# Gated linear attention into an ELU layer: a 48-column stationary operand in k·v, and a new issue order for the first ten spans

## The chip, the cores and the metric

One core of one Trainium2 chip. The metric is the time of one launch in device microseconds. Its engines are named as in the profile: PE (matmul) with its weight loads PEld, DVE, ACT, POOL, and SP, which here only issues DMAs.

## The reference

```python
for t in range(S):                    # B, H, S, D = 4, 8, 768, 48, float32
    state = alpha[:, :, t, :, None] * state + np.einsum('bhd,bhe->bhde', k[:, :, t], v[:, :, t])
    y[:, :, t] = np.einsum('bhd,bhde->bhe', q[:, :, t], state)
x = y.transpose(0, 2, 1, 3).reshape(3072, 384)
h = x @ w_in                          # w_in 384 x 2048
g = np.where(h > 0.0, h, np.exp(np.minimum(h, 0.0)) - 1.0)
out = g @ w_out                       # w_out 2048 x 384
```

## The kernel before

**Attention.** Each of the 4 batches is cut into 6 spans of 128 steps (`W`), 24 spans i in all, and each span into two chunks of 64 steps. The 8 heads lie as 4 pairs; a pair has its two heads on partitions 0 to 47 and 64 to 111. P is the running product of alpha within a span (L209, a scan on DVE), R its reciprocal (by logarithm and exponential on ACT, L218 and L223; a Newton step in L231, L236 and L241). k is divided by P, q multiplied by P. Within a chunk the scores k·q are masked and multiplied by v; across chunks a 48 x 48 state per head carries on. Its update is "k over P times v", called u, and then a multiplication by P.

**The feed-forward layer.** Two spans make a block b of 256 rows (12 blocks), and 256 hidden columns make a group j (8 groups). A group A is 18 matmuls of 128 x 256 (L655), and O is 12 matmuls of 128 x 384 (L706): every factor is split in a high and a low part, and three of the four products are formed.

**Steps and order.** The program is a list of steps; each is a name with its indices, and emits its instructions for whatever engine it uses. Every engine, and SP's DMA queue, works through its own instructions in the order of the list. There are two lists. `START` is written out by hand for spans 0 to 9 (with some steps of 10 and 11) and the first 29 of the 96 groups A. `STEADY` is one list for a group of two spans, repeated with moved indices to the end. The names that matter here, with their lines:

- LA, LB, L, LV, F: loads on SP (alpha; k and q; all three; v; weights).
- SC (L209, DVE scan), LN and EX (ACT), KA (L231) and KB (L236) on DVE or POOL, KC (L241, DVE): k over P. SQ (L258, L261): q times P.
- TP (L282, four 128 x 128 transposes on PE) with KN (L311, ACT copy) for spans 0 to 5; TA, TB, T (L292, 16, 16 and 8 transposes of 32 x 128 on DVE) from span 6 on: k with time on the partitions.
- S (L346; L330 from span 6 on): scores. MK (L363; L358): mask, on DVE.
- U (L392; L374, in the function U4, from span 6 on): u. U4 has 16 matmuls, each with one quadrant (64 x 64) of the array; the profile shows each as two records. The last span of a batch needs only half of them.
- UA, UB (L409 on ACT, L411 on DVE) and UC (L440, L442 on DVE): the state update. UP (L418): a subtraction on PE.
- YL, Y3, Y (L453, L458, L486, L497): y. XH (ACT), XP (L516, PE), XL (L534, L538 on DVE; ACT for spans 0 and 1), XD: y in two parts, the x of the next layer.
- DA (L581), DB (L587), DC (L593) on DVE: float64 words of a weight to float32, each 128 x 1536. WH (L619, ACT), WP (L628 and L516, PE), WL (L637 ACT, L639 POOL or DVE): its two parts.
- RA (L663) and RB (L668) on ACT, RC (L673, DVE), GH (L679, ACT), GL (L692, DVE): the ELU of one h and its two parts. Z (L714, L717): a block's output.

All PSUM tiles come from one pool `psa` of eight buffers, handed out in list order. A matmul into a new tile waits until the last reader of the buffer's tile before is done. The h of a group is freed by GL, its last reader.

Of the kernel before, what the change touches and what calls it, by code (L numbers as in the profile page):

```python
# [44 lines left out]


START = """
LA.0 LB.0 SC.0 LN.0 EX.0 LA.1 KA.0 KB.0 LB.1 SC.1 X.2 LV.0 LN.1 X.2 KC.0 F.2 SQ.0 EX.1 F.0 TP.0 KN.0 S.0 U.0
SQ.1 UA.0 KA.1 KB.1 MK.0 L.2 KC.1 UC.0 YL.0 LV.1 TP.1 PC.0 Y3.0 Y.0 KN.1 DA.0 PC.1 LV.2 DB.0 L.3 F.4 S.1 SC.2
U.1 XH.0 F.6 DC.0 UP.1 LN.2 XP.0 EX.2 KA.2 SQ.2 MK.1 UA.1 F.5 WH.0 WP.0 YL.1 F.1 F.3 UC.1 Y3.1 KB.2 SC.3 KC.2  # L50
WH.2 XL.0 PC.2 LN.3 DA.2 EX.3 SQ.3 Y.1 DB.2 KA.3 XH.1 TP.2 WP.2 DC.2 KB.3 KN.2 DA.1 DB.1 XP.1 KC.3 U.2 XL.1
WL.2 LC.0 WL.0 S.2 A.0.0 RA.0.0 WH.6 WL.6 F.7 A.0.1 MK.2 UB.2 UA.2 TP.3 LV.3 UC.2 S.3 L.4 KN.3 F.9 YL.2 U.3
WH.4 SC.4 WL.4 Y3.2 Y.2 UA.3 PC.3 RB.0.0 MK.3 XH.2 DA.3 SQ.4 DC.1 DB.3 YL.3 LN.4 XL.2 Y3.3 UB.3 A.0.2 LV.4
WH.3 EX.4 F.10 CA.0 F.8 WL.3 Y.3 A.0.3 XH.3 UC.3 DC.3 XL.3 L.5 F.12 RA.0.1 KA.4 KB.4 A.1.1 A.1.0 LV.5 F.11
RC.0.0 RB.0.1 RC.0.1 WH.7 GH.0.0 SC.5 DA.5 RA.0.2 GH.0.1 A.1.2 RB.0.2 DB.5 RA.1.0 KC.4 RC.0.2 WH.1 RB.1.0 F.14
GH.0.2 GL.0.0 RC.1.0 WL.1 RA.1.1 GL.0.2 A.1.3 RA.0.3 GL.0.1 RB.0.3 TP.4 UB.0 DA.4 PC.4 RB.1.1 WL.7 WH.5 KN.4
O.0.0 RC.0.3 O.0.1 GH.0.3 DB.4 U.4 WL.5 GL.0.3 RC.1.1 DC.4 RA.1.3 GH.1.1 S.4 LN.5 O.0.2 O.0.3 RB.1.3 DC.5 LV.6
L.6 WH.8 MK.4 UB.4 RA.1.2 EX.5 LV.7 GH.1.0 UA.4 RB.1.2 WL.8 GL.1.0 WH.9 KA.5 RC.1.2 CB.0 A.0.4 GH.1.2 GL.1.1
UC.4 WH.10 KB.5 RA.0.4 KC.5 O.1.0 RC.1.3 TP.5 GL.1.2 SQ.5 GH.1.3 LC.1 DA.6 CA.1 KN.5 WH.11 L.7 O.1.1 DB.6
RB.0.4 WL.10 U.5 PC.5 RC.0.4 GL.1.3 GH.0.4 UA.5 A.1.4 A.0.5 SC.6 RA.1.4 WL.11 LN.6 EX.6 KA.6 WL.9 DC.6 F.15  # L60
RB.1.4 RA.0.5 O.1.2 GL.0.4 WH.14 O.1.3 RC.1.4 RB.0.5 RC.0.5 GH.0.5 GH.1.4 S.5 KB.6 SC.7 KC.6 WH.12 Y.4 O.0.4
WL.12 GL.1.4 PC.6 LN.7 EX.7 WL.14 MK.5 GL.0.5 F.13 A.0.6 TB.6 A.0.7 CB.1 L.8 RA.0.6 A.1.5 DA.7 KA.7 TA.6 DB.7
O.0.5 XH.4 RB.0.6 RA.0.7 ZV.6 RC.0.6 RA.1.5 O.1.4 GH.0.6 XL.4 RB.0.7 Y.5 RB.1.5 KB.7 DC.7 KC.7 GL.0.6 A.1.6
WH.13 WL.13 TB.7 SQ.7 XH.5 WH.15 PC.7 XL.5 RC.0.7 RC.1.5 GH.0.7 LV.8 O.0.6 GL.0.7 TA.7 XD.4 WL.15 RA.1.6 SQ.6
RB.1.6 U.6 O.0.7 UA.6 XD.5 UB.6 UB.1 RC.1.6 GH.1.5 A.1.7 Z.0 GL.1.5 UC.6 GH.1.6 U.7 S.6 UA.7 O.1.5 SC.8 UB.7
MK.6 RA.1.7 LN.8 UC.7 A.2.4 RB.1.7 RA.2.4 GL.1.6 S.7 A.2.1 EX.8 MK.7 A.2.0 RC.1.7 Y.6 RB.2.4 RC.2.4 KA.8
RA.2.1 RB.2.1 Y.7 GH.1.7 RA.2.0 KB.8 KC.8 RB.2.0 RC.2.1 GL.1.7 L.9 SC.9 SQ.9 XH.6 XH.7 RC.2.0 GH.2.0 A.2.3
O.1.6 LN.9 TB.8 XL.7 O.1.7 A.2.5 RA.2.3 LV.10 EX.9 SQ.8 TA.8 GL.2.0 L.10 GH.2.1 KA.9 GL.2.1 U.8 PC.8 XL.6 Z.1
UA.8 S.8 XD.7 RA.2.5 A.2.2 RB.2.3 UB.8 A.2.6 UC.8 RC.2.3 KB.9 MK.8 KC.9 O.2.0 RA.2.2 RB.2.2 GH.2.4 RC.2.2 TA.9
SC.10 GH.2.2 RB.2.5 XD.6 LN.10 A.2.7 GL.2.2 GL.2.4 RA.2.6 RB.2.6 EX.10 O.2.1 RC.2.6 KA.10 GH.2.3 A.3.0 RC.2.5  # L70
RA.2.7 GL.2.3 L.11 O.2.2 LC.2 PC.9 LV.11 KB.10 RA.3.0 TB.9 O.2.3 RB.3.0 KC.10 GH.2.5 RB.2.7 GL.2.5 GH.2.6
O.2.4 RC.2.7 O.2.5 GH.2.7 RC.3.0 GL.2.6 GH.3.0 O.2.6 TA.10 S.9 GL.2.7 GL.3.0 SQ.10 LV.9 MK.9 TB.10 U.9 L.12
UA.9 UB.9 UC.9 SC.11 LN.11 EX.11 SQ.11 A.3.1 RA.3.1 RB.3.1 RC.3.1 GH.3.1 GL.3.1 O.2.7 Z.2 KA.11 KB.11 PC.10
A.3.2 RA.3.2 RB.3.2 RC.3.2 GH.3.2 CA.2 CB.2 LC.3 GL.3.2 O.3.0 KC.11 TA.11 A.3.3 RA.3.3 RB.3.3 RC.3.3 GH.3.3
CA.3 CB.3 LC.4 GL.3.3 O.3.1 TB.11 A.3.4 RA.3.4 RB.3.4 RC.3.4 GH.3.4 GL.3.4 O.3.2
"""


# [10 lines left out]
def gla_elu_ffn(ctx: ExitStack, tc: tile.TileContext, qka, vv, vn, wgt, out):  # L89
    nc = tc.nc  # L90
# [106 lines left out]
    @tok
    def V0(i):
        if EARLY <= i < QU:
            nc.sync.dma_start(out=v0[i % 2][0:64], in_=vv[i, 0:64, HD:2 * HD])  # L200
# [63 lines left out]
    @tok
    def ZS(i):
        if EARLY <= i < QS:
            for a in range(2):
                nc.gpsimd.memset(win[i]["st"][64 - 64 * a:128 - 64 * a, a], 0.0)


    @tok
# [95 lines left out]
    def U4(i):  # L367
        d = win[i]
        q4, begun = shared(i)
        d["u"] = [t[:, 0:NP * D].rearrange("p (n e) -> p n e", n=NP) for t in q4]  # L370
        for n in range(NP):
            for x, a in QUADS if i % NW < NW - 1 else QUADS[::2]:
                r = slice(64 * x, 64 * x + 64)
                nc.tensor.matmul(d["u"][x][64 * a:64 * a + 64, n, :], lhsT=d["kn"][r, n, a, :],  # L374
                                 rhs=d["vn"][r, 2 * n + a, :], start=(n == 0 and x not in begun), stop=True,
                                 skip_group_check=True)
        begun.update((0, 1) if i % NW < NW - 1 else (0,))

    @tok
    def U(i):  # L380
# [4 lines left out]
        d["u"] = [u[:, 0], u[:, 1]]
        m = 64 if i < EARLY else D
        for x in ((1, 0) if i % NW < NW - 1 else (0,)):
            r = slice(0, C) if x == 0 and i < EARLY else slice(0, 128)
            v = d["vn"] if x or i < EARLY else v0[i % 2].rearrange("p (h e) -> p h e", e=D)
            for n in range(NP):  # L390
                for a in range(2):
                    nc.tensor.matmul(d["u"][x][64 * a:64 * a + m, n, :], lhsT=d["kn"][r, n, a, 0:m],  # L392
                                     rhs=v[r, 2 * n + a, :],
                                     start=(x == int(i % NW < NW - 1) and n == 0), stop=True, skip_group_check=True)
# [573 lines left out]
```

## Time and profile before

| what | value |
|---|---|
| median of 3 runs | 504.48 us (504.24 to 504.65) |
| span of the profiled execution | 502.5 us |
| instructions in it | 13254 |
| PE, PEld busy | 98%, 95% |
| DVE, ACT, POOL busy | 77%, 58%, 26% |

The profiled execution's own time is its span and what lies before and after it: the median of the runs is about 2.0 us above the span. A row of a timeline is the start, the duration, the engine, the line, the operation, what it writes and reads, its shape, and, with x32, how many instructions the row joins; the brackets at its end hold the idle time of the engine before it and what ended that. A row of waits has the total, the count and the longest. A row of a group has, behind the first bar, its busy time and the mean ns of one. A row of a chain has only start and duration.

### The profile page before, as it was taken

Reading aid. Unit: us, or ns where it says so; the run is one execution under the profiler, and the core shown is the slowest. Engines: PE = TensorE matmul, PEld = TensorE weight load, DVE = VectorE, ACT = ScalarE, POOL = GpSimd, SP = SyncE. Lnnn points to the kernel's source line nnn. Section 1 sums busy time; section 2 is a strip of 40 time slices with the busy share of each in tenths; the row PEclk is TensorE's granted clock in tenths of the full one; section 3 lists DMA queues with packets and bytes.
Section 4 is the critical chain, followed back from the end, with each engine's and each line's share of the span. In section 5 each row is a group of like instructions: output and inputs, shape, how many; then the busy total and the mean of one; then the engine's idle time right before and its main releaser. Section 6 shows DMA issues by size and latency. Waiting matters only on the chain.

```text
span 502.5 us, 13254 instructions
## 1 busy us (share of the span) xinstructions
PE 492.4 (98%) x5404; PEld 476.0 (95%) x5404; DVE 386.6 (77%) x807; ACT 289.5 (58%) x689; POOL 129.4 (26%) x111
## 2 busy tenths in 40 slices
...
GB/s 311 412 411 382 91 95 165 64 59 100 190 59 64 57 130 178 65 83 219 54 119 178 48 119 182 63 112 172 82 112 97 95 76 44 56 42 8 3 33 36
DMA packets 22403, 61.13 MB, mean 122 GB/s; under 512 B 2880, under 2 KB 9792, under 8 KB 22336
## 3 DMA queue, kind: packets, MB, share of 16 engines
...
q8 instruction: 44, 0.72, 0.6%
...
## 4 chain that ended last, share of the span: by engine, by line
PE 96%; DVE 2%; ACT 1%; issue 1%; ACTq 0%
PE o L706 40%; PE h L655 40%; PE y L458 4%; PE y L453 2%; PE q L374 2%; PE q L330 2%; PE u L392 1%; PE sc L346 1%; PE wp L126 1%; PE y L497 1%; PE tp L282 1%; DVE kn L292 0%; PE yl L453 0%; PE wd L628 0%; DVE st L358 0%
## 5 line engine op out<-in xcount | busy, mean ns | idle before, releaser
L655 PE MATMUL h<-xt,w 128*128 128x256 f32 x1728 | 215.0, 282 | 0.0
L655 PEld LDWEIGHTS h<-xt,w 128*128 128x128 f32 x1728 | 209.3, 188 | 1.8
L706 PE MATMUL o<-w,gh 128*128 128x384 f32 x768 | 199.3, 341 | 0.6 <-ACT gh L679 0.6
L706 PEld LDWEIGHTS o<-w,gh 128*128 128x128 f32 x768 | 136.9, 188 | 1.6 <-ACT gh L679 0.8
L706 PE MATMUL o<-w,gl 128*128 128x384 f32 x384 | 130.0, 339 | 0.1
L679 ACT CAST gh<-h 128x512 fp32r<-128x512 f32 x96 | 55.9, 583 | 79.6 <-DVE h L673 39.3
L692 DVE TENSOR_TENSOR gl<-h,gh 128x512 fp32r<-128x512 f32 x96 | 65.5, 687 | 35.5 <-ACT gh L679 34.2
L292 DVE STREAM_TRANSPOSE kn<-qka 32x128 f32<-32x128 f32 x288 | 87.0, 302 | 4.5
L663 ACT ACTIVATE r<-h 128x512 f32<-128x512 f32 x96 | 57.0, 595 | 47.2 <-PE h L655 40.7
L673 DVE SCALAR_TENSOR_TENSOR h<-r,h 128x512 f32<-128x512 f32 x96 | 64.6, 689 | 16.9 <-ACT r L668 16.1
L706 PEld LDWEIGHTS o<-w,gl 128*128 128x128 f32 x384 | 72.1, 188 | 0.4 <-DVE gl L692 0.4
L231 POOL TENSOR_TENSOR qka<-qka,R 128x512 f32<-128x512 f32 x19 | 26.1, 1375 | 164.6 <-DVE gl L692 127.6
L668 ACT ACTIVATE r<-r 128x512 f32<-128x512 f32 x96 | 59.4, 631 | 0.7
L261 POOL TENSOR_TENSOR st<-qka,P 64x512 f32<-64x512 f32 x36 | 42.8, 1189 | 21.7 <-DVE P L209 16.2
L358 DVE TENSOR_TENSOR st<-q,mask 64x256 f32<-64x256 f32 x72 | 30.4, 422 | 12.0 <-ACT vs L409 9.2
L209 DVE TENSOR_TENSOR_SCAN P<-qka,first 128x516 f32<-128x516 f32 x24 | 30.6, 1275 | 1.6 <-DMA qka<-in_qka_dram 1.2
L236 POOL TENSOR_TENSOR R<-P,R 128x512 f32<-128x512 f32 x20 | 24.2, 1211 | 27.3 <-DVE qka L231 25.9
L218 ACT ACTIVATE R<-P 128x512 f32<-128x512 f32 x24 | 15.2, 632 | 27.8 <-DVE P L209 27.8
L411 DVE TENSOR_TENSOR vs<-vs,q 48x192 f32<-48x192 f32 x30 | 10.5, 350 | 19.1 <-PE q L330 16.9
L511 ACT ACTIVATE y<-y 128x128 fp32r<-128x128 f32 x20 | 5.5, 275 | 30.0 <-PE y L458 26.6
L639 POOL TENSOR_TENSOR w<-spare,w 128x768 fp32r<-128x768 f32 x7 | 15.8, 2256 | 26.0 <-ACT w L619 13.9
L611 ACT ACTIVATE ck<-ck,lim 128x384 f32<-128x384 f32 x32 | 20.6, 644 | 0.1
...
## 6 DMA issues: line engine op xcount, KB each, us to landing
...
```

The source lines that it names most:

```text
L209: nc.vector.tensor_tensor_scan(out=P.rearrange("p n w -> p (n w)"), data0=t[:, 2 * NP * W:], data1=first.rearrange("p n w -> p (n w)"), in ...
L231: eng(KAV, i).tensor_tensor(out=d["kt"], in0=d["kt"], in1=d["R"], op=ALU.mult)
L261: eng(SQV, i).tensor_tensor(out=st[r, a], in0=d["q"][r], in1=pw(i)[r], op=ALU.mult)
L292: nc.vector.transpose(out=kn[32 * t:32 * t + 32, :, 32 * g:32 * g + 32], in_=d["kt"][32 * g:32 * g + 32, :, 32 * t:32 * t + 32])
L358: nc.vector.tensor_tensor(out=d["st"][r, a, :, c * C:(c + 1) * C], in0=d["s4"][a][o], in1=mask[o].unsqueeze(1).broadcast_to([64, NP, C]), ...
L655: nc.tensor.matmul(h[:, f, :], lhsT=t[:, wi, ws], rhs=x[:, c, xi, :], start=(f == 0 and k == 0), stop=(k == 8), skip_group_check=True)
L663: nc.scalar.activation(out=r, in_=d["h"], func=AF.Relu, scale=-1.0)
L668: nc.scalar.activation(out=d["r"], in_=d["r"], func=AF.Exp, scale=-1.0)
L673: nc.vector.scalar_tensor_tensor(out=d["h"], in0=d["r"], scalar=-1.0, in1=d["h"], op0=ALU.add, op1=ALU.max)
L679: nc.scalar.copy(out=gh, in_=d["h"])
L692: nc.vector.tensor_tensor(out=gl, in0=d["h"], in1=d["gh"].bitcast(F32), op=ALU.subtract)
L706: nc.tensor.matmul(o[:, 0:DM], lhsT=gt[:, f, ms], rhs=t[:, wi, f * DM:f * DM + DM], start=(j == 0 and f == 0 and k == 0), stop=(j == NJ - ...
```

## The change

**First**, U4 takes 48 columns of k (0 to D) as its stationary operand, in place of 64, and writes 48 rows of each quadrant in place of 64; rows 48 to 63 of each quadrant hold padding, which no later step reads. **Second**, `START` is a new list of the same steps for the same spans, with a few steps more of spans 10 and 11 in another place. **Third**, the two v0 tiles, with two memsets on POOL, and the code that would use them (for no span, as `EARLY`, `QU` and `QS` are all 6) are removed. Line numbers fall by 1 from the list on and by 10 to 17 later: L209 becomes L199, L231 L221, L241 L231, L292 L275, L374 L357, L392 L375, L411 L394, L442 L425, L581 L564, L587 L570, L593 L576, L655 L638, L673 L656, L692 L675, L706 L689, and L453 L436.

```diff
@@ START @@
-LA.0 LB.0 SC.0 LN.0 EX.0 LA.1 KA.0 KB.0 LB.1 SC.1 X.2 LV.0 LN.1 X.2 KC.0 F.2 SQ.0 EX.1 F.0 TP.0 KN.0 S.0 U.0
...
+LA.0 SC.0 LN.0 LA.1 EX.0 X.2 SC.1 LB.0 KA.0 LB.1 LN.1 KB.0 LV.0 KC.0 X.2 EX.1 KA.1 TP.0 F.2 KN.0 F.0 SQ.0 SQ.1 LV.1
...
+RB.1.4 KN.5 EX.7 A.0.7 L.8 WL.12 RC.1.4 GH.0.5 RA.0.7 A.0.6 DA.7 PC.6 GH.1.4 TA.6 GL.0.5 U.5 RA.0.6 GL.1.4 UA.5
+RB.0.6 DB.7 Y.5 CB.0 RC.0.6 Y.4 DC.7 GH.0.6 XH.4 O.0.5 XH.5 GL.0.6 XL.4 WH.15 XL.5 KA.7 RB.0.7 U.6 RC.0.7 LC.1 KB.7
...
@@ gla_elu_ffn @@
-    v0 = [work.tile([128, HD], F32, name=f"v0{i}", tag=f"v0{i}", bufs=1) for i in range(2)]
-    for t in v0:
-        nc.gpsimd.memset(t, 0.0)
...
@@ U4 @@
-                nc.tensor.matmul(d["u"][x][64 * a:64 * a + 64, n, :], lhsT=d["kn"][r, n, a, :],
+                nc.tensor.matmul(d["u"][x][64 * a:64 * a + D, n, :], lhsT=d["kn"][r, n, a, 0:D],
                                  rhs=d["vn"][r, 2 * n + a, :], start=(n == 0 and x not in begun), stop=True,
@@ U @@
-            v = d["vn"] if x or i < EARLY else v0[i % 2].rearrange("p (h e) -> p h e", e=D)
+            v = d["vn"]
```

The order on DVE from the first scan on, before (qka0 and qka1 hold spans 0 and 1, raw0 a weight):

```order
L209 SCALAR_TENSOR_TENSOR P_130<-qka0_123,first_89 128x516
L231 TENSOR_TENSOR qka0_123<-qka0_123,R_132 128x512
L236 TENSOR_TENSOR R_132<-P_130,R_132 128x512
L209 SCALAR_TENSOR_TENSOR P_139<-qka1_124,first_89 128x516
L241 SCALAR_TENSOR_TENSOR qka0_123<-R_132,qka0_123 128x512
L258 TENSOR_TENSOR st_196<-qka1_124,P_139 128x512
L231 TENSOR_TENSOR qka1_124<-qka1_124,R_144 128x512
L363 TENSOR_TENSOR st_151<-sc_162,mask_85 128x2x4x64
L241 SCALAR_TENSOR_TENSOR qka1_124<-R_144,qka1_124 128x512
L442 SCALAR_TENSOR_TENSOR vs1_106<-u_179,P_130 128x192
```

and after:

```order
L199 SCALAR_TENSOR_TENSOR P_125<-qka0_119,first_89 128x516
L199 SCALAR_TENSOR_TENSOR P_133<-qka1_120,first_89 128x516
L221 TENSOR_TENSOR qka0_119<-qka0_119,R_127 128x512
L226 TENSOR_TENSOR R_127<-P_125,R_127 128x512
L231 SCALAR_TENSOR_TENSOR qka0_119<-R_127,qka0_119 128x512
L221 TENSOR_TENSOR qka1_120<-qka1_120,R_138 128x512
L248 TENSOR_TENSOR st_159<-qka1_120,P_133 128x512
L231 SCALAR_TENSOR_TENSOR qka1_120<-R_138,qka1_120 128x512
L425 SCALAR_TENSOR_TENSOR vs1_106<-u_183,P_125 128x192
```

The scan of span 1 moved ahead of KA.0, KB.0 and KC.0, and UC.0 (L442, now L425) now follows KC.1 with the mask of span 0 no longer ahead of it; ahead of UA.0 on ACT stand KN.0 and KN.1.

On PE, where U.5 stands, before (xt holds x, w1, w3 and w4 weights, o the output sums):

```order
L706 MATMUL o_978<-w1_626,gh_877 128x384 x2
L706 MATMUL o_978<-w1_626,gl_969 128x384
L392 MATMUL u_1027<-vs1_106,kn_1008 64x48 x8
L655 MATMUL h_1043<-xt_583,w4_927 128x256 x18
L655 MATMUL h_1062<-xt_292,w4_927 128x256 x18
L706 MATMUL o_977<-w3_738,gh_967 128x384 x2
```

and after, without the buffer numbers of the program:

```order
L689 MATMUL o<-w_969,gl 128x384
L638 MATMUL h<-xt,w_985 128x256 x36
L375 MATMUL u<-vs_106,kn 64x48 x8
L436 MATMUL y<-st,vs_106 64x64 x32
L436 MATMUL y<-st,vs_105 64x64 x32
L689 MATMUL o<-w_969,gh 128x384 x2
```

U.5 moved behind A.0.7 and A.0.6, and Y.5 and Y.4 follow it at once. The DVE instructions ahead of these, in the list after (kn is k of span 6, gl and h belong to the layer, raw7 to a weight):

```order
L231 SCALAR_TENSOR_TENSOR qka0_119<-R_1014,qka0_119 128x512
L275 STREAM_TRANSPOSE kn_1149<-qka0_119 32x4x32 x8
L656 SCALAR_TENSOR_TENSOR h_1016<-r_1127,h_1016 128x512
L564 TENSOR_SCALAR wm_1208<-raw7_1113 128x1536
L275 STREAM_TRANSPOSE kn_1149<-qka0_119 32x4x32 x8
L675 TENSOR_TENSOR gl_1221<-h_1038,gh_1185 128x512
L675 TENSOR_TENSOR gl_1234<-h_1016,gh_1211 128x512
L394 TENSOR_TENSOR vs1_106<-vs1_106,u_1223 128x192
```

where before has this at the same work:

```order
L241 SCALAR_TENSOR_TENSOR qka0_123<-R_1086,qka0_123 128x512
L692 TENSOR_TENSOR gl_1200<-h_1043,gh_1130 128x512
L363 TENSOR_TENSOR st_999<-sc_1132,mask_85 128x2x4x64
L692 TENSOR_TENSOR gl_1208<-h_1062,gh_1128 128x512
L292 STREAM_TRANSPOSE kn_1230<-qka0_123 32x4x32 x8
L581 TENSOR_SCALAR wm_1281<-raw7_1092 128x1536
L292 STREAM_TRANSPOSE kn_1230<-qka0_123 32x4x32 x8
```

Both halves of span 6's transposes now stand ahead of the two gl (GL.0.5 and GL.1.4) and of UA.5 (L394); before, the two gl stood ahead of the transposes.

More of the change, by code (lines that the diff above doesn't have):

```diff
@@ L47 @@
 START = """
-LA.0 LB.0 SC.0 LN.0 EX.0 LA.1 KA.0 KB.0 LB.1 SC.1 X.2 LV.0 LN.1 X.2 KC.0 F.2 SQ.0 EX.1 F.0 TP.0 KN.0 S.0 U.0
[L49 to L72, printed above, removed]
@@ L73 @@
-UA.9 UB.9 UC.9 SC.11 LN.11 EX.11 SQ.11 A.3.1 RA.3.1 RB.3.1 RC.3.1 GH.3.1 GL.3.1 O.2.7 Z.2 KA.11 KB.11 PC.10
-A.3.2 RA.3.2 RB.3.2 RC.3.2 GH.3.2 CA.2 CB.2 LC.3 GL.3.2 O.3.0 KC.11 TA.11 A.3.3 RA.3.3 RB.3.3 RC.3.3 GH.3.3
-CA.3 CB.3 LC.4 GL.3.3 O.3.1 TB.11 A.3.4 RA.3.4 RB.3.4 RC.3.4 GH.3.4 GL.3.4 O.3.2
+LA.0 SC.0 LN.0 LA.1 EX.0 X.2 SC.1 LB.0 KA.0 LB.1 LN.1 KB.0 LV.0 KC.0 X.2 EX.1 KA.1 TP.0 F.2 KN.0 F.0 SQ.0 SQ.1 LV.1
+KB.1 L.2 KC.1 S.0 LV.3 U.0 TP.1 PC.0 KN.1 UA.0 PC.1 UC.0 L.3 DA.0 MK.0 DB.0 S.1 U.1 F.4 UP.1 YL.0 MK.1 UA.1 YL.1 F.6
```

32 lines of the change are left out of this document (23 added, 9 removed).

## The prediction

> **What bounds the kernel now.** I read the page's first part and its chain first, then the waits of PE, then the busy time in five stretches.
>
> ```profile
> PE 492.4 (98%) x5404; PEld 476.0 (95%) x5404; DVE 386.6 (77%) x807; ACT 289.5 (58%) x689; POOL 129.4 (26%) x111
> ...
> PE 96%; DVE 2%; ACT 1%; issue 1%; ACTq 0%
> ```
>
> ```profile
> PE wp L126 <- DVE first L120: 2.1, 1, 2.1
> PE tp L282 <- issue: 1.7, 1, 1.7
> PE o L706 <- ACT gh L679: 0.6, 1, 0.6
> ```
>
> ```profile
> core 0: us, PE busy (x) PEld busy (x) DVE busy (x) ACT busy (x) POOL busy (x), PEclk, DMA share, GB/s
> 9.50:30.00 20.50, 19.46 (x364) 15.97 (x365) 19.06 (x22) 12.80 (x34) 2.73 (x2) 1.00 1.02 413
> 30.00:100.00 70.00, 70.00 (x835) 67.76 (x836) 67.25 (x95) 45.05 (x94) 38.42 (x22) 1.00 0.52 188
> 100.00:165.00 65.00, 65.00 (x738) 63.50 (x735) 57.55 (x137) 31.09 (x70) 19.82 (x17) 1.00 0.29 91
> 165.00:180.00 15.00, 14.26 (x150) 13.54 (x149) 8.78 (x21) 11.09 (x27) 4.99 (x6) 1.00 0.18 56
> 180.00:450.00 270.00, 270.00 (x2988) 265.71 (x2987) 211.84 (x489) 166.78 (x427) 58.68 (x50) 1.00 0.34 107
> ```
>
> PE is the bound: its work alone fills the span, and its named waits are single ones of 2.1 us or less. So the time changes in two ways only: by less work on PE, or by other idle time of PE. But from 9.5 to 100 DVE is nearly as full (19.06 of 20.50 and 67.25 of 70.00 us). There PE and DVE run neck and neck, and an order that sends a DVE result a little later makes PE wait. From 180 on DVE has slack (211.84 of 270.00) and that part's order is unchanged.
>
> **Part 1: the narrower stationary operand.** The bursts of L374 (spans 6 to 23), the bursts of L330 between them, and bursts of other shapes:
>
> ```profile
> 260.86 0.68 PE L374 MATMUL q<-vs,kn 64*64 64x48 f32 x32
> 261.37 0.66 PE L330 MATMUL q<-st,qka 48*64 48x64 f32 x32
> ```
>
> ```profile
> L374 PE MATMUL q<-vs,kn 64*64 64x48 f32 x528 | 11.9, 220 | 0.0
> ```
>
> ```profile
> 23.17 1.60 PE L453 MATMUL y<-st,vs 48*48 48x64 f32 x48
> ```
>
> ```profile
> 83.55 2.08 PE L453 MATMUL y<-st,vs 48*64 48x64 f32 x64
> ```
>
> ```profile
> 55.18 0.60 PE L282 MATMUL tp<-ident,qka 128*128 128x128 f32 x4
> ```
>
> The 32 records of one burst start within 0.68 − 0.22 = 0.46 us, so eight sets of four quadrants go at about 0.46/8 = 58 ns a set. x528 is 15 spans of 32 and three (11, 17, 23) of 16, in all 18 × 8 = 144 sets. What a set costs at 48 columns no row shows. From the one side: y with a 48-column stationary operand and 64 moving columns takes (1.60 − 0.22)/47 = 29.4 ns a record, with 64 and 64 (2.08 − 0.22)/63 = 29.5 ns; shortening one operand while the other is at 64 gave nothing, so the gain here may be 0. Here, however, v is already 48 wide and the 64 columns are the only long side left. From the other side: the 128-wide transposes come every (0.60 − 0.28)/3 = 107 ns, so the slope from 64 to 128 is (107 − 58)/64 = 0.77 ns a column, 12.2 ns for 16 columns, 144 × 12.2 = 1.76 us. Strictly in proportion to the columns it would be 58 × 16/64 × 144 = 2.1 us. The rows nearest are the transposes and L374 itself, where both sides of the larger operand are seen; a straight line through 64 and 128 flattens to a fixed part below, so I take a little less than 1.76: **−1.5 us** (0 to −2.1).
>
> A rule of the Trainium skill speaks for less ("TensorE: Matmul & The Clock Gate", section "Wait — 56ns, not 53.3ns?"): matmuls never start closer than about 25 ns, however small. Two such steps to a set would leave 50 ns, an estimate of 144 × 8 = 1.15 us from that page; by it the forecast would be 0.35 us later. The 29.4 ns above agree with it as far as they go; no run here shows a record at the floor.
>
> The deleted tiles, memsets and loads of v0 are two POOL memsets at the very start and code that no span reaches. They cost nothing either way: POOL is 26% busy.
>
> **Part 2: the new order at the start.** DVE, PE and ACT as they now start:
>
> ```profile
> 3.61 1.23 DVE L209 TENSOR_TENSOR_SCAN P<-qka,first 128x516 f32<-128x516 f32 x1 [0.72 <-DMA qka<-in_qka_dram]
> 6.30 0.69 DVE L231 TENSOR_TENSOR qka<-qka,R 128x512 f32<-128x512 f32 x1 [1.45 <-ACT R L223]
> ...
> 7.63 1.23 DVE L209 TENSOR_TENSOR_SCAN P<-qka,first 128x516 f32<-128x516 f32 x1
> 8.77 0.67 DVE L241 SCALAR_TENSOR_TENSOR qka<-R,qka 128x512 f32<-128x512 f32 x1
> ```
>
> ```profile
> 9.54 0.63 PE L282 MATMUL tp<-ident,qka 128*128 128x128 f32 x4 [1.68 <-issue]
> 10.20 0.58 ACT L311 COPY kn<-tp 128x512 f32<-128x512 f32 x1
> 12.56 0.33 ACT L409 ACTIVATE vs<-u 128x192 f32<-128x192 f32 x1 [1.77 <-PE u L392]
> ```
>
> The second scan (1.23 us) moves into DVE's hole of 1.45 us before 6.30, if its load has landed. KC.0 (L241) then starts at 7.63 and ends at 8.30, and the first transposes start 0.1 later, at 8.4 for 9.54: −1.1 us for PE. The load of the second half of k's span 0 (LB.0) moves behind another load in SP's queue; KA.0 needs it at 6.30. Given back: UC.0 (L425) now follows KC.1 on DVE directly, but needs UA.0, and UA.0 on ACT stands behind KN.1, which needs TP.1. From KC.1's end that is 0.10 + 0.63 (TP.1) + 0.03 + 0.58 (KN.1) + 0.33 (UA.0) = 1.7 us of idle DVE, which was zero there. Queued behind UC.0 are the weight steps DA.0, DB.0 and everything after them. UB.2 waits for U.2 too, at most one burst:
>
> ```profile
> 27.11 1.20 PE L392 MATMUL u<-vs,kn 128*64 128x48 f32 x29
> ```
>
> so 0 to 1.2 us, taken at 0.75. For PE the start is worth between −1.1 and 0; I take −0.5, since TP.1 and U.0 follow earlier but the DVE work behind UC.0 comes later.
>
> **Part 3: U.5 and Y.5, the place that decides.** After the change PE has, behind A.0.7 and A.0.6, U.5 (L375), Y.5, Y.4 and then O.0.5. The only free PSUM bank for U.5 is the one that holds h of (0,5), which GL.0.5 on DVE reads last. Y.5 needs UA.5 (L394), which stands behind GL.0.5 and GL.1.4. Ahead of these two DVE has TB.6, DA.7 and TA.6. In the profile of before, PE reaches A.0.6 and DVE does the same transposes here:
>
> ```profile
> 29.32 4.47 PE h L655 x36
> ...
> 87.95 6.34 PE h L655 x54
> ```
>
> ```profile
> 89.70 2.49 DVE L292 STREAM_TRANSPOSE kn<-qka 32x128 f32<-32x128 f32 x8
> 92.23 1.76 DVE L587 SCALAR_TENSOR_TENSOR wm<-raw,wm 128x1536 int32<-128x1536 int32 x1
> 93.90 0.69 DVE L673 SCALAR_TENSOR_TENSOR h<-r,h 128x512 f32<-128x512 f32 x1
> 94.50 0.28 DVE L534 TENSOR_TENSOR y<-y,y 128x128 fp32r<-128x128 f32 x1
> 94.70 0.55 DVE L538 TENSOR_TENSOR xt<-y,xt 128x384 fp32r<-128x384 f32 x1
> 95.16 1.75 DVE L593 SCALAR_TENSOR_TENSOR wm<-raw,wm 128x1536 int32<-128x1536 int32 x1
> ...
> 97.43 0.69 DVE L692 TENSOR_TENSOR gl<-h,gh 128x512 fp32r<-128x512 f32 x1
> ```
>
> ```profile
> 37.06 0.35 DVE L411 TENSOR_TENSOR vs<-vs,u 128x192 f32<-128x192 f32 x1 [0.21 <-PE u L392]
> ```
>
> DVE: up to GL.0.5, the changed order holds exactly the instructions that before has done at 89.70 + 2.49 = 92.19, less one L411 (0.35) and one L692 (0.69): 91.15 at equal idle time. Before's idle time on DVE up to there is about 5.0 us: 1.45 at 6.30, 1.44 between 9.5 and 30, and most of the 2.75 between 30 and 100. Of these:
>
> ```profile
> DVE h L673 <- ACT r L668: 0.9, 1, 0.9
> DVE spare L581 <- issue: 0.6, 1, 0.6
> ```
>
> After it is 0.2 left of the first hole, 1.7 and 0.75 from above, and what stays of the rest, 0 to 3.5, taken at 1.8, half: 4.45 in all. GL.0.5 so ends at 91.15 − 0.55 = **90.6** (88.9 to 92.5). GL.1.4 (0.69) and UA.5 (0.35) follow, so Y.5 starts at 91.7.
>
> PE: at 87.95 before has done 11 h groups, 9 output groups, U.0 to U.5 and Y.0 to Y.4. The new order has, ahead of Y.5, the same with two more h groups (2 × 6.34/3 = 4.2) and without Y.4 (2.0, from 83.55 above). Before was that far at 87.95 + 4.2 − 2.0 = 90.15. Without any wait the new order would be there 0.5 earlier, at 89.65; it gets there at 91.7. So it has lost **+1.5 us** against before at Y.5 (0 or less if GL.0.5 ends by 89.1, +3.4 if at 92.5).
>
> Next: Y.5, Y.4 and O.0.5 take PE 2.1 + 2.0 + 2.1 = 6.2, to 97.9. U.6 and A.1.6 need banks or data behind DB.7, RC.0.6, DC.7, GL.0.6, XL.4 and XL.5: 1.76 + 0.69 + 1.75 + 0.69 + 2 × (0.28 + 0.55) = 6.55 after 91.65, 98.2: **+0.3 us**.
>
> One stall of before goes. The last PE wait of the hand-written order:
>
> ```profile
> 167.17 0.70 DVE L673 SCALAR_TENSOR_TENSOR h<-r,h 128x512 f32<-128x512 f32 x1 [2.61 <-ACT r L668]
> ...
> 168.54 0.62 PE L706 MATMUL o<-w,gh 128*128 128x384 f32 x2 [0.63 <-ACT gh L679]
> ```
>
> There A.3.1 stands right ahead of the output products that need it. The new list issues A.3.3, A.3.1, A.3.0 and A.3.2 spread out, several groups ahead of their O, so the 15.00 − 14.26 = 0.74 us of idle PE between 165 and 180 should go: **−0.7 us**. I see nothing late next: behind it stands the unchanged repeating part, where DVE is 78% busy.
>
> Sum: +1.5 + 0.3 − 0.7 = +1.1 for the order, −1.5 for the operand, together −0.4. The profiled execution's span is 502.5 and the median 504.48, about 2.0 outside the span; the span becomes 502.1, the time **504.1 us**.
>
> **The rivals.** A difference under 0.2% (1.0 us) can't be told from none in this kernel.
> - *DVE is early enough* (0.33). If the 0.9, 0.6 and the like don't recur, GL.0.5 ends before 89.1 and PE never waits for it: −0.5 − 0.7 − 1.5 = −2.7, **501.8 us**. For it: before's DVE waits depend on an order that is gone. Against it: two new waits of DVE that the order forces.
> - *The bank of U.5 costs more* (0.15). Two more waits like the 0.9 on DVE and GL.0.5 ends at 92.5: +3.4 at Y.5, then +0.3 and −0.7, −1.5: +1.5, **506.0 us**. It decides from about 92.0 on (+2.9 at Y.5), the point from which the sum is over +1.0. For it: DVE has only 2.75 us of slack between 30 and 100, so nothing that is late there is made up.
> - *The narrower operand gives nothing* (0.10), as the y rows allow: 504.48 + 1.1 = **505.6 us**.
>
> **How the numbers follow.** The forecast's own case has 0.42, with 503.1 to 505.1 as its own range (GL.0.5 a microsecond either way). Faster than 503.47: nearly all of the first rival's 0.33 less 0.05, and 0.09 of the forecast's: 0.37. Slower than 505.49: 0.14 of the second rival, half of the third's 0.10 and 0.03 of the forecast's: 0.22. The rest, 0.41, is same. The range 501.6 to 506.1 leaves out the lower third of the first rival and the upper half of the second, about 0.18.
>
> **What would show it.** Right: in the profile after, PE waits once between 88 and 93 for a DVE L675 or L394 by 1.5 to 2.6 us, DVE waits about 1.7 us ahead of its first L425, TP.0 starts near 8.4, a burst of L357 lasts about 0.37 for 0.46 us from first start to last, and there is no wait of PE near 167. Wrong: no PE wait at U.5 or Y.5 (first rival), further waits of PE between 40 and 110 (second), starts of L357 still 58 ns a set apart (third), or waits in the repeating part, which I hold unchanged.

## The result: 4% slower

The changed kernel takes 525.38 us (median of 4, 523.33 to 528.29), the kernel before 504.56 in the same comparison; the ratio is 1.0407, with a 95% interval of 1.0365 to 1.045. The forecast was 504.1, the top of its range 506.1, and none of the rivals reaches this far. Every ratio below leaves out slow runs, of which there were two: 548.27 us at a granted clock of 0.842 (the transposes moved behind GL.0.5) and 1220.6 us (operand and safe start together).

The page of the profile after, first part and granted clock in 40 slices (the span is 526.6 us):

```profile
PE 503.9 (96%) x5404; PEld 484.7 (92%) x5404; DVE 402.9 (77%) x807; ACT 289.3 (55%) x689; POOL 135.2 (26%) x109
...
PEclk8599899799999999999999999999999999999999
```

Three things stand out. PE is busy 11.5 us longer (503.9 for 492.4) with the same 5404 records. DVE is busy 16.3 us longer (402.9 for 386.6) with the same 807 instructions. And the granted clock, which was full in every stretch shown of before, has dips in the first quarter. The busy time in three stretches of the profile after:

```profile
core 0: us, PE busy (x) PEld busy (x) DVE busy (x) ACT busy (x) POOL busy (x), PEclk, DMA share, GB/s
10.00:30.00 20.00, 18.93 (x277) 16.49 (x277) 12.88 (x17) 6.56 (x17) 1.56 (x1) 0.57 1.01 404
30.00:110.00 80.00, 71.04 (x749) 66.85 (x748) 77.88 (x87) 45.04 (x93) 42.52 (x23) 0.94 0.43 157
110.00:526.00 416.00, 407.99 (x4364) 399.37 (x4364) 306.17 (x694) 233.78 (x574) 86.65 (x71) 1.00 0.30 91
```

Between 10 and 30 the mean granted clock is 0.57: 20 × 0.43 = 8.6 us of PE's full speed are missing, idle time included. Between 30 and 110 it is 0.94 (80 × 0.06 = 4.8 us), and PE also idles 80.00 − 71.04 = 9.0 us there, where before had none. DVE is full (77.88 of 80.00).

The waits of PE in the profile after:

```profile
PE tp L265 <- issue: 4.4, 1, 4.4
PE tp L265 <- DVE qka L231: 3.5, 2, 3.1
PE tp L265 <- DVE gl L675: 3.4, 1, 3.4
...
PE o L689 <- DVE gl L675: 1.0, 2, 0.7
PE q L357 <- DVE kn L275: 1.0, 2, 0.6
PE h L638 <- DVE st L341: 0.8, 1, 0.8
PE u L375 <- DVE gl L675: 0.8, 1, 0.8
```

Every one of these waits ends with DVE (that of 4.4 us, put down to "issue", ends 0.1 us after KC.4 on DVE, below). Their places in PE's timeline:

```profile
11.07 1.09 PE L265 MATMUL tp<-ident,qka 128*128 128x128 f32 x4 [3.09 <-DVE qka L231]
12.08 1.97 PE L329 MATMUL sc<-st,qka 48*64 48x64 f32 x32
...
28.44 1.60 PE L436 MATMUL y<-st,vs 48*48 48x64 f32 x48
...
58.61 1.09 PE L265 MATMUL tp<-ident,qka 128*128 128x128 f32 x4 [4.41 <-issue]
...
96.70 1.11 PE L265 MATMUL tp<-ident,qka 128*128 128x128 f32 x4 [3.44 <-DVE gl L675]
...
110.36 0.67 PE L375 MATMUL u<-vs,kn 64*64 64x48 f32 x16 [0.76 <-DVE gl L675]
110.96 4.00 PE L436 MATMUL y<-st,vs 48*64 48x64 f32 x128
...
117.19 0.57 PE L357 MATMUL q<-vs,kn 64*48 64x48 f32 x32
```

After each long wait the same four transposes take 1.1 us instead of 0.6: the wait itself is paid once, and then again at half clock. The granted clock is 0.50 throughout these three stretches, which begin within the three waits, and full between them:

```profile
10.11:27.18 17.07, 16.11 (x206) 14.00 (x208) 10.91 (x14) 4.33 (x11) 1.56 (x1) 0.50 1.00 401
57.90:61.31 3.41, 2.70 (x10) 2.73 (x11) 3.41 (x5) 1.15 (x3) 0.06 (x1) 0.50 1.01 416
95.45:102.27 6.82, 5.57 (x44) 5.13 (x45) 6.79 (x9) 5.18 (x12) 6.67 (x5) 0.50 0.21 64
```

PE is busy 16.11 + 2.70 + 5.57 = 24.4 us in them. At full clock this work would take about half (an estimate from the granted clock), so the half clock cost up to 12.2 us. After the first stretch, at 28.44, y takes its 1.60 us again.

DVE in the same execution, at the start and ahead of TP.4:

```profile
7.96 0.69 DVE L221 TENSOR_TENSOR qka<-qka,R 128x512 f32<-128x512 f32 x1 [1.95 <-DMA qka<-in_qka_dram]
8.69 1.55 DVE L226 TENSOR_TENSOR R<-P,R 128x512 f32<-128x512 f32 x1
...
18.03 0.36 DVE L425 SCALAR_TENSOR_TENSOR vs<-u,P 128x192 f32<-128x192 f32 x1 [4.10 <-ACT vs L392]
...
48.94 2.59 DVE L576 SCALAR_TENSOR_TENSOR spare<-raw,spare 128x1536 int32<-128x1536 int32 x1
...
53.04 3.26 DVE L570 SCALAR_TENSOR_TENSOR wm<-raw,wm 128x1536 int32<-128x1536 int32 x1
...
56.69 1.82 DVE L231 SCALAR_TENSOR_TENSOR qka<-R,qka 128x512 f32<-128x512 f32 x1
...
109.61 1.29 DVE L675 TENSOR_TENSOR gl<-h,gh 128x512 fp32r<-128x512 f32 x2
```

and POOL at those times:

```profile
8.01 1.68 POOL L248 TENSOR_TENSOR st<-qka,P 128x512 f32<-128x512 f32 x1 [4.38 <-DMA qka<-in_qka_dram]
...
48.73 1.19 POOL L226 TENSOR_TENSOR R<-P,R 128x512 f32<-128x512 f32 x1
52.48 5.48 POOL L622 TENSOR_TENSOR w<-spare,w 128x768 fp32r<-128x768 f32 x2 [2.56 <-ACT w L602]
```

L226 takes 1.55 us while SQ.0 runs on POOL, 0.69 without it; L570 takes 3.26 and KC.4 (L231) 1.82 while two WL run on POOL, 1.76 and 0.67 without. POOL's two WL take 5.48 together, where the shortest in this trace takes 1.83. By groups, after and then before:

```profile
L675 DVE TENSOR_TENSOR gl<-h,gh 128x512 fp32r<-128x512 f32 x96 | 65.4, 687 | 41.6 <-ACT gh L662 40.4
L231 DVE SCALAR_TENSOR_TENSOR qka<-R,qka 128x512 f32<-128x512 f32 x24 | 20.2, 845 | 1.2 <-POOL R L226 1.1
L570 DVE SCALAR_TENSOR_TENSOR wm<-raw,wm 128x1536 int32<-128x1536 int32 x4 | 9.4, 2360 | 0.0
L564 DVE TENSOR_SCALAR wm<-raw 128x1536 int32<-128x1536 int32 x4 | 6.1, 1526 | 0.0
```

```profile
L241 DVE SCALAR_TENSOR_TENSOR qka<-R,qka 128x512 f32<-128x512 f32 x24 | 16.7, 695 | 0.3 <-POOL R L236 0.2
L587 DVE SCALAR_TENSOR_TENSOR wm<-raw,wm 128x1536 int32<-128x1536 int32 x4 | 7.0, 1758 | 0.1
L581 DVE TENSOR_SCALAR wm<-raw 128x1536 int32<-128x1536 int32 x4 | 4.5, 1114 | 0.0
```

The instructions that grew have all their operands in SBUF. GL (L675), which reads h in PSUM, has the same 687 ns in both. This suggested the theory that the runs below test: POOL and DVE exclude each other while both read SBUF, and the new order makes DVE the loser more often.

### The profile page after: what moved, and what is told of

Read it like the earlier page. It is cut to its first block, busy times and chain, and to the rows that moved or that the text cites. A ratio compares the mean times of both kernels' runs of the same rounds, so it can differ in the third digit from the quotient of the medians.

```text
span 526.6 us, 13263 instructions
## 1 busy us (share of the span) xinstructions
PE 503.9 (96%) x5404; PEld 484.7 (92%) x5404; DVE 402.9 (77%) x807; ACT 289.3 (55%) x689; POOL 135.2 (26%) x109
## 4 chain that ended last, share of the span: by engine, by line
PE 64%; DVE 4%; issue 1%; ACT 0%; DVEq 0%; ACTq 0%
PE o L689 30%; PE h L638 28%; PE y L441 3%; DVE kn L275 3%; PE q L313 1%; PE q L357 1%; DVE gl L675 1%; DVE qka L231 0%; DVE h L656 0%; ACT gh L662 0%; ACT ot L697 0%; DVE vs L423 0%; PE vd L730 0%; DVEq L517 0%; DVE P L199 0%
## 5 line engine op out<-in xcount | busy, mean ns | idle before, releaser
L638 PE MATMUL h<-xt,w 128*128 128x256 f32 x1728 | 214.3, 282 | 0.8 <-DVE st L341 0.8
L638 PEld LDWEIGHTS h<-xt,w 128*128 128x128 f32 x1728 | 209.2, 188 | 2.9 <-PE y L441 0.9
L689 PE MATMUL o<-w,gh 128*128 128x384 f32 x768 | 201.0, 343 | 0.0
L689 PEld LDWEIGHTS o<-w,gh 128*128 128x128 f32 x768 | 138.3, 190 | 0.9
L689 PE MATMUL o<-w,gl 128*128 128x384 f32 x384 | 130.8, 341 | 1.0 <-DVE gl L675 1.0
L675 DVE TENSOR_TENSOR gl<-h,gh 128x512 fp32r<-128x512 f32 x96 | 65.4, 687 | 41.6 <-ACT gh L662 40.4
L275 DVE STREAM_TRANSPOSE kn<-qka 32x128 f32<-32x128 f32 x288 | 87.1, 303 | 4.5
L656 DVE SCALAR_TENSOR_TENSOR h<-r,h 128x512 f32<-128x512 f32 x96 | 64.8, 688 | 17.0 <-ACT r L651 16.1
L689 PEld LDWEIGHTS o<-w,gl 128*128 128x128 f32 x384 | 72.8, 189 | 1.7 <-DVE gl L675 1.7
L221 POOL TENSOR_TENSOR qka<-qka,R 128x512 f32<-128x512 f32 x19 | 26.0, 1367 | 186.2 <-DVE gl L675 118.0
L251 POOL TENSOR_TENSOR st<-qka,P 64x512 f32<-64x512 f32 x36 | 46.5, 1292 | 13.6 <-DVE P L199 11.8
L199 DVE TENSOR_TENSOR_SCAN P<-qka,first 128x516 f32<-128x516 f32 x24 | 32.9, 1377 | 1.4 <-DMA qka<-in_qka_dram 0.8
L226 POOL TENSOR_TENSOR R<-P,R 128x512 f32<-128x512 f32 x20 | 24.2, 1212 | 28.7 <-DVE qka L221 27.3
L394 DVE TENSOR_TENSOR vs<-vs,q 48x192 f32<-48x192 f32 x30 | 10.5, 348 | 15.7 <-PE q L313 15.0
L231 DVE SCALAR_TENSOR_TENSOR qka<-R,qka 128x512 f32<-128x512 f32 x24 | 20.2, 845 | 1.2 <-POOL R L226 1.1
```

The source lines that it names most:

```text
L199: nc.vector.tensor_tensor_scan(out=P.rearrange("p n w -> p (n w)"), data0=t[:, 2 * NP * W:], data1=first.rearrange("p n w -> p (n w)"), in ...
L221: eng(KAV, i).tensor_tensor(out=d["kt"], in0=d["kt"], in1=d["R"], op=ALU.mult)
L275: nc.vector.transpose(out=kn[32 * t:32 * t + 32, :, 32 * g:32 * g + 32], in_=d["kt"][32 * g:32 * g + 32, :, 32 * t:32 * t + 32])
L638: nc.tensor.matmul(h[:, f, :], lhsT=t[:, wi, ws], rhs=x[:, c, xi, :], start=(f == 0 and k == 0), stop=(k == 8), skip_group_check=True)
L656: nc.vector.scalar_tensor_tensor(out=d["h"], in0=d["r"], scalar=-1.0, in1=d["h"], op0=ALU.add, op1=ALU.max)
L675: nc.vector.tensor_tensor(out=gl, in0=d["h"], in1=d["gh"].bitcast(F32), op=ALU.subtract)
```

## The experiments

**The operand alone, and the order alone.**

```diff
 (before)
-    nc.tensor.matmul(d["u"][x][64 * a:64 * a + 64, n, :], lhsT=d["kn"][r, n, a, :],
+    nc.tensor.matmul(d["u"][x][64 * a:64 * a + D, n, :], lhsT=d["kn"][r, n, a, 0:D],
 (after: the reverse)
```

> The kernel before with the 48-column operand alone, old order. Theory 1 (the operand is a gain and the whole loss is the order's): 18 bursts, each 95 ns shorter from first to last start (370 in place of 463 ns in the profile after), 1.7 us less: 502.8 us, 0.9966. Rival (the narrower operand upsets something, for example the clock): 510 us or more.

> The new order with the 64-column operand. Theory 1: the loss stays, 525.4 + 1.7 = 527 us. Rival (the loss needs the narrower operand): near 504 us.

The operand alone: 504.28 us beside 504.94, ratio 0.9999 (0.9978 to 1.0021): not to be told from nothing. Three of its twelve runs took 507.4 to 508.6 us, at a mean clock of 0.988 to 0.995; they weigh on the ratio and hardly on the median. The new order alone: 524.69, ratio 1.0395 (1.0371 to 1.0418). So the loss is the order's.

**The start.** A step X.n is n of the matmuls that PE does at the start into a tile nobody reads ("idle matmuls"). First the old order of the first 15 steps in the changed kernel, then 12 more idle matmuls to keep PE busy, then the reverse in the kernel before: four idle matmuls fewer.

```diff
 (after, first run)
-LA.0 SC.0 LN.0 LA.1 EX.0 X.2 SC.1 LB.0 KA.0 LB.1 LN.1 KB.0 LV.0 KC.0 X.2 EX.1 KA.1
+LA.0 LB.0 SC.0 LN.0 EX.0 LA.1 KA.0 KB.0 LB.1 SC.1 X.2 LV.0 LN.1 X.2 KC.0 EX.1 KA.1
 (after, second run)
-... KC.0 X.2 EX.1 KA.1
+... KC.0 X.14 EX.1 KA.1
 (before)
-... SC.1 X.2 LV.0 LN.1 X.2 KC.0 ...
+... SC.1 LV.0 LN.1 KC.0 ...
```

> The changed kernel with the first 15 steps in the order of before (second load of span 0 right behind the first, second scan behind KB.0); all behind them as changed. Theory A (the late load makes PE idle for 3 us, and the half clock from 11 to 28 us follows from that): first transposes at 9.5, granted clock 1.00 up to 40 us, at least half of 17 us back, 515 us or less. Theory B (the loss is made between 40 and 110 us, by DVE instructions that POOL stretches and by waits of PE for them): the start mends but 5 to 10 us more are lost later, 513 to 518 us. Rival (the start costs nothing, since DVE is late later anyway): 522 us or more.

> The changed kernel with 12 more of the idle matmuls that PE does at the start (they write a tile nobody reads), ahead of the first transposes: these still start at 11.1 us, but PE is busy until about 10.5. If the half clock comes from the idle 3.1 us: clock 1.00 from 10 to 30 us, some 8 us back, 517 us. If it has another cause (the work itself, the load): no change, 525 us.

> The kernel before without the last 4 of the 16 idle matmuls ahead of the first transposes, so that PE idles 3.2 us there in place of 1.7. If an idle time of 3 us drops the granted clock: 0.5 from 9.5 us on for 10 us or more, and 4 to 8 us longer, 509 to 513. If the half clock of the changed kernel's start had another cause: 504.5 us.

The old head gives 525.87 us (ratio 1.0391, 1.0362 to 1.042): no gain. Its first transposes did start earlier, but the clock was halved all the same, after an idle time of only 1.99 us:

```profile
10.00 0.92 PE L265 MATMUL tp<-ident,qka 128*128 128x128 f32 x4 [1.99 <-issue]
```

So this run did not separate what it was meant to. The idle matmuls keep the clock full at the start in their profile (1.00 between 10 and 30 us), but the time is 523.76, not 517 (ratio 1.0364, 1.0341 to 1.0388). The kernel before with fewer of them idles 2.5 us there, has this row for the stretch from 9 to 20 us, and takes 508.78 us beside 505.12 (ratio 1.0068, 1.0045 to 1.0091):

```profile
9.00:20.00 11.00, 10.09 (x135) 8.73 (x137) 8.36 (x10) 4.32 (x11) 1.18 (x1) 0.55 1.02 415
```

So a cold start alone is worth about 3.7 us, which fits the changed kernel's own runs: two at a mean clock of 0.973 and 0.974 (528.29 and 527.05 us), two at 0.986 and 0.987 (523.33 and 523.72). Some 19 us have another cause.

**POOL's work taken away, in the new order and in the old.** Both leave out the WL steps of POOL and let the matmuls read the high part of these weights twice; the new order also has the 12 idle matmuls. WLV lists the weights whose WL runs on DVE, WPE those whose second part PE makes; the others are POOL's.

```diff
-        else:
+        elif f in WLV:
             eng(WLV, f).tensor_tensor(out=wgts[f][:, 1], ...
...
-  nc.tensor.matmul(h[:, f, :], lhsT=t[:, wi, ws], ...
+  nc.tensor.matmul(h[:, f, :], lhsT=t[:, wi if 2 * j in WPE + WLV else 0, ws], ...
```

> The kernel of the run with 12 more idle matmuls, with the weight steps WL that POOL does left out (the matmuls read the high part in place of the low one, so the output is not the reference's; PE's work is the same in number and shape). Theory C (POOL's tensor operations stretch DVE's instructions that have all operands in SBUF, and the new order lays more of them side by side): the stretch of DVE between its second L576 and the end of the transposes of span 6 falls from 16.4 to under 7 us, these transposes end near 95 in place of 104, PE's waits of 4.4 and 3.1 us go, and the time is 508 to 512 us. Rival (DVE is late by the order itself, the stretch is incidental): 520 us or more.

> The control of the run without WL, on the kernel before: the weight steps WL that POOL does are left out, the matmuls read the high part in place of the low one, and the output is not the reference's. Theory C: DVE gets freer here too (stretch 7.2 to about 2 us), but PE is the bound, so the time stays at 504 to 505 us; the 10 us gained in the new order come from the collisions that it makes. Rival (POOL's work costs any order about the same): 495 to 500 us.

"Stretch" in these texts is the sum, over DVE's instructions, of what each takes beyond the usual time of its shape. In the new order the time falls from 523.76 to 513.69 us (ratio to before 1.0158, 1.0104 to 1.0213), in the old one it stays: 504.40 (0.9981, 0.9959 to 1.0003). DVE's busy time in the new order with all steps (12 idle matmuls), without WL, and in the old order without WL:

```profile
PE 500.8 (96%) x5416; PEld 481.8 (92%) x5416; DVE 403.3 (77%) x807; ACT 288.8 (55%) x689; POOL 135.6 (26%) x109
```

```profile
PE 497.8 (97%) x5416; PEld 479.5 (93%) x5416; DVE 391.2 (76%) x807; ACT 288.3 (56%) x689; POOL 105.6 (21%) x96
```

```profile
PE 491.5 (98%) x5404; PEld 475.6 (95%) x5404; DVE 385.4 (77%) x807; ACT 289.3 (58%) x689; POOL 102.8 (20%) x98
```

DVE does the same 807 instructions in all three. Without WL on POOL they take 12.1 us less in the new order, but only 1.2 less than the 386.6 of before in the old one. Of PE's waits of 4.4 and 3.1 us, which the run with all steps still had, the first is 1.1 and the second is gone. What remains in the new order without WL is the place that the prediction had picked:

```profile
94.58 1.09 PE L375 MATMUL u<-vs,kn 64*64 64x48 f32 x16 [2.21 <-DVE gl L675]
95.47 6.57 PE L436 MATMUL y<-st,vs 48*64 48x64 f32 x128
```

PE waits 2.2 us at U.5 for GL.0.5, as forecast, and then does Y.5 and Y.4 at half clock: 6.57 us, where the profile after has 4.00 for the same 128 records. The 513.69 us are 1.7 us above the 512 expected at most.

**POOL's work added, in the old order.** First every WL on POOL twice, then instead three memsets ahead of each WL, together about as long as one.

```diff
 (first)
-            eng(WLV, f).tensor_tensor(...)
+            for _ in range(1 if f in WLV else 2):
+                eng(WLV, f).tensor_tensor(...)
 (second)
+            for n in () if f in WLV else (WCH, WCH, 280):
+                nc.gpsimd.memset(wgts[f][:, 1, 0:n].bitcast(F32), 0.0)
             eng(WLV, f).tensor_tensor(...)
```

> The kernel before, with every WL on POOL done twice (the same result written again). Theory C: about 10 more POOL operations of 1.8 to 2.4 us before 105 us stretch DVE by some 0.7 us each, 6 to 9 us in all; DVE has 2.75 us of slack there, so PE waits and the time grows by 4 to 10 us, to 509 to 515. Rival (POOL's work does not matter to DVE): 505 to 506 us.

> The kernel before, where each WL on POOL is preceded by three memsets of its own target (768, 768 and 280 columns, some 1.8 us; the WL then overwrites them). POOL is as late as in the run with WL twice, but the added work reads no SBUF operand. Theory C in its narrow form (what stretches DVE is a POOL operation that reads SBUF operands): DVE's stretch up to span 6's transposes stays near 7 us, against 20.6 with WL twice; PE's direct waits for POOL remain, and the time is 508 to 515 us. Rival (POOL being late is the whole loss of that run, or any POOL work stretches DVE): stretch 15 us or more or the time at 522 to 525.

WL twice: 524.25 us (ratio 1.0376, 1.0321 to 1.0432), more than expected; with memsets 514.39 (1.0172, 1.0128 to 1.0216). The pages and waits for POOL, first with WL twice, then with memsets:

```profile
PE 500.3 (96%) x5404; PEld 480.9 (92%) x5404; DVE 401.2 (77%) x807; ACT 289.9 (56%) x689; POOL 161.6 (31%) x124
```

```profile
PE o L707 <- POOL w L640: 5.5, 3, 3.0
...
PE h L656 <- POOL w L640: 1.8, 2, 1.3
```

```profile
PE 496.9 (97%) x5404; PEld 478.3 (93%) x5404; DVE 392.2 (77%) x807; ACT 289.7 (57%) x689; POOL 152.2 (30%) x150
```

```profile
PE o L708 <- POOL w L641: 2.7, 1, 2.7
PE h L657 <- POOL w L641: 2.3, 2, 1.3
```

Neither run is pure: PE also waits for the late WL itself (7.3 and 5.0 us). But WL twice makes DVE's 807 instructions 14.6 us longer than before, the memsets 5.6 us, with POOL 32 and 23 us busier. What stretches DVE is mainly a POOL operation that reads SBUF, not POOL's being busy. Up to the end of span 6's transposes DVE is busy 84.6 us before, 99.0 with WL twice and 90.0 with memsets. The memsets were expected to add nothing there and add 5.4 us; that the WL, which are still there, now fall on other DVE instructions would explain it, but is not shown.

**WL on DVE.**

```diff
-WLV, KAV, KBV, SQV = (0, 4), ...
+WLV, KAV, KBV, SQV = tuple(range(16)), ...
```

> The new order with 12 more idle matmuls, with every WL on DVE in place of POOL (0.93 us each there, 1.8 or more on POOL). Theory C, with a lock that one engine holds while the other stands still: about 10 us less stretch of DVE, about 10 us more work, so the end of span 6's transposes stays within 2 us of 104.1 and the time at 521 to 526. Rival (POOL's work beside DVE is for the most part free): DVE 8 to 10 us later, 530 us or more.

523.20 us (ratio 1.0349, 1.0313 to 1.0386), as the theory has it, beside 523.76 with WL on POOL; span 6's transposes end at 104.5, beside 104.1. The page has this:

```profile
PE 499.5 (96%) x5416; PEld 480.2 (92%) x5416; DVE 402.9 (77%) x820; ACT 289.1 (55%) x689; POOL 106.8 (20%) x96
```

13 more instructions, and DVE's busy time is 402.9 in place of 403.3. In the new order, giving WL to POOL saved DVE nothing: what it no longer did, it stood still for.

**The transposes behind GL.0.5.** In the new order with 12 idle matmuls, TB.6 and TA.6 were moved behind UA.5.

```diff
-... LN.7 TB.6 F.15 ...
-... GH.1.4 TA.6 GL.0.5 U.5 RA.0.6 GL.1.4 UA.5
+... LN.7 F.15 ...
+... GH.1.4 GL.0.5 U.5 RA.0.6 GL.1.4 UA.5 TB.6 TA.6
```

> The kernel of the run with 12 more idle matmuls, with both halves of span 6's transposes moved behind GL.0.5, GL.1.4 and UA.5. The recorded prediction (this place decides): PE's wait at U.5 of 0.8 to 1.8 us goes, and 1 to 2 us with it: 522 us for 523.8. If DVE's lateness there is much larger than these transposes, the wait only moves to U.6: no change, 523.5 to 524.

Three runs took 526.65 to 530.46 us (ratio 1.0461, 1.0378 to 1.0543), each longer than all four without the move (522.99 to 524.74). Neither expectation held. The wait at U.5 went, and one at U.6, the next step that needs DVE, took its place and grew:

```profile
115.22 0.39 PE L357 MATMUL q<-vs,kn 64*48 64x48 f32 x2 [4.09 <-DVE gl L675]
```

**Operand and a safe start together**, on the kernel before:

```diff
-    nc.tensor.matmul(d["u"][x][64 * a:64 * a + 64, n, :], lhsT=d["kn"][r, n, a, :],
+    nc.tensor.matmul(d["u"][x][64 * a:64 * a + D, n, :], lhsT=d["kn"][r, n, a, 0:D],
...
-... SC.1 X.2 LV.0 LN.1 X.2 KC.0 ...
+... SC.1 X.2 LV.0 LN.1 X.8 KC.0 ...
```

> The kernel before with the 48-column operand and 6 more idle matmuls ahead of the first transposes, so that PE's idle time of 1.7 to 2.0 us there shrinks to 0.5. Theory 1: the 1.7 us of the operand show, without now and then a half clock at the start: 503 us, 0.997. Rival (the bursts' gain is lost elsewhere): 504.5 us.

504.14 us beside 504.97, ratio 0.9986 (0.9967 to 1.0005). The median is 0.8 us lower, nearer to the rival's 504.5 than to 503, and the interval holds 1: no version here is shown to beat the kernel before.

## Why the prediction was wrong

**The step that failed** is in its part 3: "up to GL.0.5, the changed order holds exactly the instructions that before has done at 89.70 + 2.49 = 92.19 ...: 91.15 at equal idle time". The count is right; that equal instructions take equal time is not. GL.0.5 ended at 110.3 and not at 90.6. These stretches end with that work, in before and in the changed kernel, then in the new order with 12 more idle matmuls, with and without WL (in the last three the 115th DVE instruction is GL.1.4, just begun):

```profile
0.00:92.20 92.20, 87.45 (x1122) 78.22 (x1123) 84.61 (x116) 56.55 (x123) 43.78 (x38) 1.00 0.70 262
0.00:110.31 110.31, 95.86 (x1040) 85.33 (x1040) 97.00 (x115) 55.77 (x116) 48.58 (x38) 0.88 0.56 212
0.00:104.83 104.83, 91.48 (x1052) 80.91 (x1052) 97.08 (x115) 56.74 (x118) 49.02 (x38) 0.95 0.59 223
0.00:94.53 94.53, 87.15 (x1052) 77.28 (x1052) 86.27 (x115) 56.63 (x119) 24.22 (x27) 1.00 0.66 247
```

Before's work, less the 0.35 and 0.69 of the two instructions that are not there yet, is 83.57 us, and the forecast end of 90.6 leaves 7.0 us of idle time. In the changed kernel the same work took 97.00 us, 13.4 more, and DVE idled 13.3 us. With the 12 idle matmuls, at full clock at the start, DVE idled 7.75 us, nearly as forecast, and GL.0.5 still ended at 104.83: 13.5 of the 14.2 us of lateness are longer instructions. Without WL only 2.7 us are, and it ended at 94.53.

The instructions are longer because in the new order POOL's WL, KA and SQ run beside DVE's SBUF-only instructions (weight steps, scans, KC), and one stands still for the other. Taking WL away gave 10.1 us back in the new order and none in the old: this is shown. The row of before that could have warned stands in the prediction: between 30 and 100 us DVE has 2.75 us of slack, so any such stretch reaches PE.

The Trainium skill states the mechanism ("SBUF — State Buffer", section "Who interferes with whom"): a DVE instruction with two SBUF inputs contends with a GpSimd instruction that reads SBUF, not with one that only writes it, and the one that issues first blocks the other until it is done. The runs here agree: 14.6 us of longer DVE work with WL twice, 5.6 with memsets. L564, which has a single input, grew too (1114 to 1526 ns); the rule on two inputs does not cover it.

**The clock** was missing altogether. The prediction priced a wait of PE at its own length. After waits of 3.09, 4.41 and 3.44 us PE went on at half clock, and the up to 12.2 us worked out above are about as much as the idle time itself: from the page, PE's idle time grew by 526.6 − 503.9 − (502.5 − 492.4) = 12.6 us and its busy time by 11.5, together the 24.1 us by which the spans differ (the operand takes 1.6 to 1.7 us off the busy time). The cold start alone was tried on the kernel before, at 3.7 us; the half clock after the later waits could not be taken away by itself, so its share is read from the profile only.

Point by point:

- *PE is the bound, DVE runs neck and neck with it to 100 us*: right, and the second half decided.
- *The operand, −1.5 us*: its mechanism was right. A burst's 32 records now start within 0.57 − 0.20 = 0.37 us, not 0.46, so 18 bursts save 1.6 to 1.7 us, and the third rival's sign, starts still 58 ns a set apart, did not show. At the 46 ns a set that this makes, a step (one of two matmuls a set) is 23 ns, a little under the 25 ns that the Trainium skill gives as a floor ("TensorE: Matmul & The Clock Gate", section "Wait — 56ns, not 53.3ns?"). In the time, at most 0.7 to 0.8 us of it show, within the interval.
- *First transposes at 8.4*: wrong. LB.0, moved behind another load, held KA.0 until 7.96, and KB.0 took 1.55 for 0.69 us beside SQ.0 on POOL. They started at 11.07 in the profile shown; in that of the new order with the 64-column operand KA.0 started at 6.28 and they at 9.38, so the load's delay varies, and KB.0's 1.55 us does not.
- *UC.0 idles DVE 1.7 us*: right in kind. It was 4.10 us in the profile shown, with PE at half clock, and 1.60 with the 12 idle matmuls, at full clock.
- *U.5 waits for GL.0.5, about 2 us*: right in place and size once most of DVE's stretch is away (2.21 us without WL), the size in part by luck: DVE came 3.9 us later than forecast (94.5 for 90.6), and PE 3.3 us later (92.4 for about 89.1). In the changed kernel PE had by then lost so much that only 0.76 were left there.
- *The stall near 167 goes, −0.7*: it went, but between 120 and 210 us PE has seven waits for DVE of 0.3 to 0.8 us, 3.5 us together, where before has only that stall of 0.63. Two of them (at 207.76 and 208.41, 1.0 us together, the L357 for L275 in the rows above) lie in the repeating part, which the prediction held unchanged.
- *The rival "DVE is early enough"* needed GL.0.5 by 89.1; it came at 110.3.
- *The rival "The bank of U.5 costs more"* had the sign and the engine, and the point that nothing late on DVE is made up; its price of 506.0 lacked both the longer instructions and the half clock.

What stays open: by medians the new order without WL is still 8.6 us above before (513.69 and 505.12), and 11 us by the spans of the profiles. In its profile 80.00 − 76.65 = 3.35 us of idle PE between 30 and 110 and a clock of 0.96 there (3.2 us) are part of it, and the same seven waits behind 110, 3.5 us. These were not tried one by one. And why DVE rather than POOL loses more often in the new order was not traced step by step.
